# Gated linear attention and a squared-ReLU network on one core: float32 products by fewer sub-products, or by three single-pass products of exact parts

## The chip, the cores and the metric

The kernel runs on one NeuronCore of a Trainium2 chip. The metric is the device time of one execution in microseconds, lower is better. The profile gives a span a little shorter than that time: from the first to the last instruction of the core.

## The reference

Two stages follow each other. Inputs are four tensors of 4 batches, 8 heads, 768 steps and 48 channels in float32, and two weight matrices in float64 that the kernel itself turns into float32.

```python
for t in range(S):                                   # attention, S = 768
    state = alpha[:, :, t, :, None] * state + np.einsum('bhd,bhe->bhde', k[:, :, t], v[:, :, t])
    y[:, :, t] = np.einsum('bhd,bhde->bhe', q[:, :, t], state)
x = y.transpose(0, 2, 1, 3).reshape(B * S, H * D)    # 3072 tokens x 384
h = np.maximum(x @ w_in, 0.0)                        # 384 -> 2048
out = h * h @ w_out                                  # 2048 -> 384
```

The output is float32, 3072 x 384.

## The kernel before

Time is cut into 6 chunks of 128 steps. A block is one chunk of one batch, all heads, so there are 24 blocks. Four blocks, one of each batch, form a group of 512 tokens, and the feed-forward network runs group by group (g = 0 to 5). Attention of a group is made while the network of the group before runs.

*Attention of a block.* ACT takes the logarithm of alpha (`ln`), DVE splits it in two FP32R parts (`sp`, from block 8 on), TensorE sums the logs over time (`cs`, L267 and L268, FP32R matmuls of 384 columns), ACT makes exponentials (`eb`, `ei`), DVE scales q and k (`mq`, `mk`), TensorE transposes both (`turn`, L532) and ACT copies them (`turned_copied`, L540). Then `ga` and `gb` work on halves of 64 steps: `scores` (L421), `state_sums` (L447), masks and state updates on DVE, and the products y (L397). `ev` copies y from PSUM into x, the network's input.

*Feed-forward, group 0.* `ffn_in` and `ffn_out` are plain float32 matmuls (L723, 512 columns; L742, 384 columns). In this group the weights arrive and are converted from float64 on DVE and ACT.

*Feed-forward, groups 1 to 5.* `layer_in` follows a written list, LAYER. It computes the first layer with sub-products of sums of blocks: W_SUMS and X_SUMS say which blocks of the weights and of x are added or subtracted, a word such as `Pu0=w11x9` is one sub-product (two matmuls of 256 columns, L674), and words such as `u3=b1` or `u6=u3-b3` combine the results on ACT or DVE (L698, L616). The list has 40 sub-products where plain blocks would need 48. `ffn_product` does the same for the second layer with seven products instead of eight (PRODUCTS, L780, matmuls of 192 columns), with sums of weights (`tsum`) and of the hidden values (`sums`).

*Order of the work.* The schedule is manual: the order of the statements is the order of each engine's queue. `weave` goes through a list of units, each with a cost, and puts an event in when the sum of costs reaches the event's time. `attention` turns the table PLAN into events; in groups 1 to 4 they are all woven into `ffn_product`, with none in `layer_in`. PSUM has eight banks: `ps_att` holds four, `ps_ffn` four. x lives in one fixed buffer `x_t`, the hidden values in eight fixed buffers `hid`.

Of the kernel before, what the change touches and what calls it, by code (L numbers as in the profile page):

```python
# [17 lines left out]
GB = 4  # L18

# [6 lines left out]
def kernel(  # L26
# [25 lines left out]
    nc = tc.nc  # L52
# [16 lines left out]
    ps_att = ctx.enter_context(tc.tile_pool(name="ps_att", bufs=4, space=PSUM))  # L69
    ps_ffn = ctx.enter_context(tc.tile_pool(name="ps_ffn", bufs=GB, space=PSUM))  # L70
# [18 lines left out]
    w_in_t = consts.tile([128, NW, KM, DF // NW], FP32, name="w_in")  # L89
    w_in = [w_in_t[:, i] for i in range(NW)]  # L90
    w_out = [consts.tile([128, NJ // NW, DM], FP32, name=f"w_out{i}") for i in range(NW)]
    HM, NR2 = DM // 2, NJ // 4
    tsum = [kept(f"t{i}_", NR2, [128, 2, HM]) for i in (1, 2, 4)]
# [6 lines left out]
    lent = {("a", 2): flat(tsum[0][0]), ("a", 3): flat(tsum[0][1])}  # L100
    for x, n, i in (("q", 2, 6), ("q", 3, 7), ("k", 3, 5)):
        t = lent[x, n] = flat(w_out[i])[:, 0 : 64 * H].rearrange("a (h d) -> a h d", h=H)
        nc.gpsimd.memset(t[:, :, D:64], 0.0)
# [18 lines left out]
    def load_weights(i):  # L122
        dst = (w_in + w_out)[i]
        dt = moe_w_in.dtype
        raw = dst if dt == FP32 else raw_pool.tile(list(dst.shape), dt, tag="raw", name="raw")
        raws[i] = raw
        if i < NW:
            src = moe_w_in[:, i * DF // NW : (i + 1) * DF // NW]
            nc.sync.dma_start(out=raw, in_=src.rearrange("(k r) f -> r k f", r=128))
        else:  # L130
            i -= NW
            src = moe_w_out[i * DF // NW : (i + 1) * DF // NW, :]
            nc.sync.dma_start(out=raw, in_=src.rearrange("(j r) m -> r j m", r=128))
# [5 lines left out]

    def convert_first(i):  # L140
        if moe_w_in.dtype == FP32:
            return
        w = (w_in + w_out)[i].rearrange("a k f -> a (k f)")
# [4 lines left out]
        power = cv_pool.tile([128, n], U32, tag="power", name="power")  # L148
# [79 lines left out]
    x_t = consts.tile([128, KM, GB * C], FP32, name="x")  # L228
    xs_t = consts.tile([128, 11, HT], FP32, name="xs")
    hid = [consts.tile([128, 2, GB * C], FP32, name=f"hid{i}") for i in range(NJ // 2)]  # L230

    def bank(n, name, shape=(NP, C)):

        if n < GB and name in ("sc", "y"):
            return ps_ffn.tile([128, *shape], FP32, tag="f", name=name)
        return ps_att.tile([128, *shape], FP32, tag="att", name=name)
# [271 lines left out]
    def gb(a, n):  # L508
# [10 lines left out]
        if a is not None:  # L519
            ev(a)  # L520
            for m in (a, a + 1):
                blk[m].clear()
# [19 lines left out]
    def ev(n):  # L542
        g, t = divmod(n, GB)
        if t == 0:
            xT[g] = x_t
        x = xT[g].rearrange("a k (t c) -> a k t c", c=C)

        for p in range(NP):
            for e, f, end in ((1, 2 * p * D + 32, 2 * (p + 1) * D), (0, 2 * p * D, (2 * p + 1) * D)):
                copy = nc.vector.tensor_copy if n in SHARED and e else nc.scalar.copy  # L550
                r = 64 * (e ^ p % 2)
                while f < end:
# [3 lines left out]
                        out=x[to : to + m, kk, t : t + 2],  # L556
# [3 lines left out]
        blk[n].pop("y")  # L560

    def st(n):
# [25 lines left out]
    W_SUMS = """  # L588
        12=8+6 6=6-3 13=5-8 2=13-2 14=1-2 5=14+5 11=5+11 15=11-1 11=11+10 5=5+3 16=11+3 9=16+9
        3=8+3 10=9-10 1=1-10 17=11+4 4=4-14 18=0-1 0=3-0 19=11+7  # L590
    """
    X_SUMS = """
        6=4-0 7=6+5 8=1-7 9=8+3 10=4-2 11=10+5 12=5+4 13=9+6 14=3-11 15=14+1 16=9+2
    """

    LAYER = """
        Pu0=w11x9 Pv1=w8x6 Pu2=w8x6 u3=b1 Pv3=w3x7 v3=b2 Pv4=w11x9 u6=u3-b3 Pu5=w3x7 u1=u6+b4
        Pu6=w16x8 v3=v3-b5 Pu7=w13x5 u2=v3+b0 Pv4=w13x5 u5=b6-u2 Pv0=w16x8 u3=u5+b7 Pu6=w17x3  # L600
        v5=b0-u1 Pu7+w14x11 u0=v5+b4 Pu0=w5x12 u3=u3+b6 Pu5+w0x0 u7=v3-b7 v0=b0 Pv6=w17x3 V+u3
        Pu7+w2x10 v3=u0+b6 Pv1+w12x0 Rv3=+v3 u0=v0-b7 Pu6=w15x13 Qv3 u0=u0-b5 Pv4+w14x11 Ru0=+u0
        v0=u5+b6 Pu7+w1x15 Qu0 v2=u6-b4 Pu6+w9x16 u6=b7-u2 Pv5=w5x12 u6=u6-b0 Pv4+w2x10 u6=u6+b6
        u2=b5 Pu0+w4x2 Ru6=+u6 v4=u2-b4 Pu7+w10x14 Qu6 u2=u7+b0 Pv6=w15x13 Ru2=+u2 u7=v0+b7
        Pv4+w1x15 Qu2 v7=v5+b6 Pv3+w0x0 Ru7=-u7 u1=b4-u1 Pu7+w18x1 Qu7 v6=u1-b5 Pv1+w7x2 Su1
        Ru1=+b7 Pv4+w10x14 v0=v4-b3 Qu1 Pv6+w9x16 Rv4=+b1 V+v0 Pv5+w4x2 Qv4 v7=v7+b4 Pu2+w12x0
        v6=v6+b6 Rv7=-v7 v2=v2+b5 Pv0=w19x3 Qv7 V+v6 Rv2=+v2 Pv0+w6x1 Sv1 Qv2 Pu2+w7x2 v5=v5+b0
        Pu7=w19x3 Ru4=+b2 V+v5 Pu7+w6x1 Qu4 Pv4+w18x1 u5=u5+b7 V+u5 Rv1=+b4 Qv1 Su0 Sv0
    """
    FIRST = "u"  # L610

    acc, ws, sums = {}, {}, {}
# [5 lines left out]
    def parsed(text):  # L618
        for word in text.split():
            o, x, op, z = re.fullmatch(r"(\d+)=(\d+)([+-])(\d+)", word).groups()  # L620
            yield int(o), int(x), ALU.add if op == "+" else ALU.subtract, int(z)

    def w_slot(i):
        if i < 4 * KM:
            c, kk = divmod(i, KM)
            return w_in_t[:, 2 * c : 2 * c + 2, kk, :]
        r, i = divmod(i - 4 * KM, 3)
        if r not in ws:
            ws[r] = raw_pool.tile([128, 3, 2, 256], FP32, tag="raw", name="ws")
            if r == 2:  # L630
                sums.update({3: ws[r][:, 2]})
        return ws[r][:, i]

    def x_slot(i):
        kk, h = divmod(i, 2)
        return x_t[:, kk, h * HT : (h + 1) * HT] if kk < KM else xs_t[:, i - 2 * KM]

    w_sums = list(parsed(W_SUMS))

    def sum_w_in(i):  # L640
        o, x, op, z = w_sums[i]
        combine(((w_slot(o), w_slot(x), op, w_slot(z)),))

    def sum_x(g):
        if not xs_ready:
            a = raw_pool.tile([128, 3, 2, HT], FP32, tag="raw", name="s012")
            sums.update({r: a[:, r] for r in range(3)})
            xs_ready.append(True)
        for o, x, op, z in parsed(X_SUMS):
            combine(((x_slot(o), x_slot(x), op, x_slot(z)),))  # L650

    xs_ready = []

    def part(name):
        c, h = divmod(int(name[1]), 2)
        return hid[2 * c + "uv".index(name[0])][:, :, h * HT : (h + 1) * HT]

    def layer_in(g, between):
        banks = {}

        def operand(name):
            return banks[name[1]] if name[0] == "b" else part(name)

        for n, word in enumerate(LAYER.split()):
            if n in between:
                between[n]()
            if word[0] == "P":
                p, b, start, w, x = re.fullmatch(r"P([uv])(\d)([=+])w(\d+)x(\d+)", word).groups()
                if start == "=":
                    banks.pop(b, None)  # L670
                    pool, tag = ((ps_att, "att"), (ps_ffn, "f"))[int(b) // 4]
                    banks[b] = pool.tile([128, 2, HT], FP32, tag=tag, name="h")
                for i in range(2):
                    nc.tensor.matmul(  # L674
                        out=banks[b][:, i, :],
                        lhsT=w_slot(int(w))[:, "uv".index(p), i * 128 : (i + 1) * 128],
                        rhs=x_slot(int(x)), start=(start == "=" and i == 0), stop=True,
                        skip_group_check=True,
                    )
            elif word[0] == "S":  # L680
                r = 2 * int(word[2]) + "uv".index(word[1])
                combine(((sums[r], halves(r)[1], ALU.add, halves(NR2 + r)[1]),))
            elif word[0] == "V":
                t = part(word[2:])
                nc.vector.scalar_tensor_tensor(
                    out=t, in0=t, scalar=0.0, in1=t,
                    op0=ALU.max if word[1] == "+" else ALU.min, op1=ALU.mult,
                )
            elif word[0] == "Q":
                t = part(word[1:])  # L690
                nc.scalar.activation(out=t, in_=t, func=AF.Square)  # L691
            elif word[0] == "R":
                o, sign, x = word[1:3], word[4], word[5:]
                nc.scalar.activation(  # L694
                    out=part(o), in_=operand(x), func=AF.Relu, scale=1.0 if sign == "+" else -1.0
                )
            elif len(word) == 5:
                nc.scalar.copy(out=part(word[0:2]), in_=operand(word[3:5]))  # L698
            else:
                o, x, op, z = word[0:2], word[3:5], word[5], word[6:8]  # L700
                combine(((
                    part(o), operand(x), ALU.add if op == "+" else ALU.subtract, operand(z)
                ),))
# [272 lines left out]
```

## Time and profile before

| what | value |
|---|---|
| time, median of 3 executions | 551.77 us (548.78 to 1417.08) |
| profiled execution | 549.13 us, span 547.4 us |
| granted TensorE clock | 0.998 |
| PE busy | 534.2 us (98%) |
| DVE busy | 368.6 us (67%) |
| ACT busy | 235.8 us (43%) |
| moved by DMA | 37.02 MB, 108820 of 117085 packets under 512 B |

How to read the profile: busy time of PE counts a matmul from its start to its modelled end, so neighbours overlap, and the start-to-start distance is the true price of a matmul in a stream. A float32 matmul has two records, each with its load of weights (PEld). The slices cut the span into 40 equal parts and give the busy share in tenths. The chain of work follows back from the last instruction what released what. The five `layer_in` stages begin at 132.96, 222.97, 307.84, 392.34 and 472.28 us.

### The profile page before, as it was taken

What the parts mean: (1) busy time and instruction counts of PE and PEld (TensorE: products, weight loads), DVE (VectorE), ACT (ScalarE), POOL (GpSimd) and SP (SyncE); (2) the same over time, 40 slices, a digit from 0 to 9 for tenths busy, and PEclk for the clock granted to TensorE, in tenths of its full rate; (3) what the DMA queues carried; (4) which work ended last, traced back from release to release, by engine and by line L of the source; (5) the groups of instructions that cost most, each with busy time, mean ns of one, the idle gap of its engine ahead of it and who ended that gap; (6) DMA issues with size and microseconds to landing.
All of it is one profiled execution on the core that took longest, in us unless ns stands there. A gap on an engine that the chain in (4) does not pass through costs nothing.

```text
span 547.4 us, 12320 instructions
## 1 busy us (share of the span) xinstructions
PE 534.2 (98%) x5226; PEld 455.3 (83%) x5226; DVE 368.6 (67%) x656; ACT 235.8 (43%) x503; POOL 5.9 (1%) x26
## 2 busy tenths in 40 slices
PE   8889999999999999999999999999999999999996
PEld 5654456656889999989999988999988999988996
DVE  4888889993898873778583677673578651577530
ACT  4568874435264354246343236542326440336100
POOL 2010000000000000000000000000000000000000
PEclk9999999999999999999999999999999999999999
DMA  9979577201001664200343300252300000100001
GB/s 162 239 191 278 148 225 204 59 16 57 1 1 30 118 112 88 66 1 0 60 90 63 85 0 1 46 94 55 88 1 0 2 2 2 57 1 0 1 1 57
DMA packets 117085, 37.02 MB, mean 68 GB/s; under 512 B 108820, under 2 KB 111912, under 8 KB 117032
## 3 DMA queue, kind: packets, MB, share of 16 engines
q1 hardware_dynamic: 117032, 36.25, 29.5%
q8 instruction: 41, 0.67, 0.5%
q14 instruction: 12, 0.10, 0.1%
HBM read 31.49 MB, written 4.75 MB: 66 GB/s over the span
## 4 chain that ended last, share of the span: by engine, by line
PE 81%; DVE 10%; ACT 4%; issue 2%; DMA 2%; SPq 0%; POOL 0%; DVEq 0%; POOLq 0%
PE o L780 33%; PE h L674 32%; PE o L742 4%; PE y L397 4%; PE sckv L421 2%; PE T L532 2%; PE sckv L447 2%; ACT power L163 1%; DMA raw<-in_moe_w_in_dram 1%; DVE w_out L176 1%; DMA raw<-in_moe_w_out_dram 1%; DVE power L172 1%; DVE power L150 1%; DVE w_in L176 1%; DVE w_out L179 1%
## 5 line engine op out<-in xcount | busy, mean ns | idle before, releaser
L616 DVE TENSOR_TENSOR hid<-hid,h 128x512 f32<-128x512 f32 x130 | 88.4, 687 | 40.5 <-PE h L674 37.0
L780 PE MATMUL o<-w_out,hid 128*128 128x192 f32 x480 | 82.3, 327 | 0.0
L780 PEld LDWEIGHTS o<-w_out,hid 128*128 128x128 f32 x480 | 78.5, 190 | 0.6
L674 PE MATMUL h<-xs,w_in 128*128 128x256 f32 x320 | 74.8, 379 | 0.0
L555 ACT COPY x<-y 32x256 f32<-32x256 f32 (+2 forms) x132 | 46.3, 365 | 59.7 <-PE y L397 56.1
L674 PEld LDWEIGHTS h<-xs,w_in 128*128 128x128 f32 x320 | 60.7, 190 | 8.3
L674 PE MATMUL h<-x,ws 128*128 128x256 f32 x200 | 49.7, 379 | 0.0
L723 PE MATMUL h<-x,w_in 128*128 128x512 f32 (+1 forms) x108 | 43.5, 550 | 3.3 <-ACT x L555 1.8
L431 DVE COPY_PREDICATED am<-halves_mask,sckv 128x256 f32<-128x256 uint32 x40 | 15.5, 441 | 43.7 <-PE sckv L447 43.7
L698 ACT COPY hid<-h 128x512 f32<-128x512 f32 x20 | 11.7, 586 | 76.7 <-PE h L674 76.7
L780 PE MATMUL o<-t,s 128*128 128x192 f32 x240 | 43.2, 328 | 0.0
L742 PE MATMUL o<-w_out,hid 128*128 128x384 f32 x128 | 42.8, 490 | 0.0
L674 PEld LDWEIGHTS h<-x,ws 128*128 128x128 f32 x200 | 38.0, 190 | 5.2
L674 PE MATMUL h<-x,w_in 128*128 128x256 f32 x160 | 40.2, 379 | 0.0
L780 PEld LDWEIGHTS o<-t,s 128*128 128x128 f32 x240 | 39.5, 190 | 0.3
L723 PEld LDWEIGHTS h<-x,w_in 128*128 128x128 f32 x108 | 20.0, 190 | 23.4 <-issue 16.3
L742 PEld LDWEIGHTS o<-w_out,hid 128*128 128x128 f32 x128 | 23.9, 190 | 16.2 <-issue 0.5
L691 ACT ACTIVATE hid<-hid 128x512 f32<-128x512 f32 x55 | 34.7, 631 | 1.8
L674 PEld LDWEIGHTS h<-x,w_in 128*128 128x128 f32 x160 | 30.4, 190 | 4.1
L674 PE MATMUL h<-xs,ws 128*128 128x256 f32 x120 | 30.0, 379 | 0.0
L694 ACT ACTIVATE hid<-hid 128x512 f32<-128x512 f32 x35 | 22.0, 628 | 16.9 <-DVE hid L616 16.6
L780 PE MATMUL o<-t,hid 128*128 128x192 f32 x160 | 28.8, 331 | 0.0
(128 smaller groups left out, 764.8 us busy)
## 6 DMA issues: line engine op xcount, KB each, us to landing
raw<-in_moe_w_in_dram SPq DMA_DIRECT2D x8, 768.0 KB
raw<-in_moe_w_out_dram SPq DMA_DIRECT2D x8, 768.0 KB
v_in<-in_v_dram SPq DMA_DIRECT2D x24, 192.0 KB
out_dram<-osb SPq DMA_DIRECT2D x24, 192.0 KB
k_in<-in_k_dram SPq DMA_DIRECT2D x23, 192.0 KB
a_in<-in_alpha_dram SPq DMA_DIRECT2D x22, 192.0 KB
q_in<-in_q_dram SPq DMA_DIRECT2D x22, 192.0 KB
last<-row SPq DMA_DIRECT2D x40, 0.8 KB
```

What stands on the lines that cost most here:

```text
L176: nc.vector.scalar_tensor_tensor(out=w, in0=upper, scalar=2.0**-20, in1=w, op0=ALU.mult, op1=ALU.add)
L397: ins = nc.tensor.matmul(out=ys[e][64 * half : 64 * half + D + G * e, m % 2, p // 2, t], lhsT=lhsT, rhs=rhs, start=(half, e) not in seen, ...
L431: nc.vector.copy_predicated(out=am_h(n)[:, e, n % 2], data=ps[e][:, 0], mask=halves_mask.bitcast(U32).unsqueeze(1).to_broadcast([128, NP, ...
L555: copy(out=x[to : to + m, kk, t : t + 2], in_=blk[n]["y"][e][r : r + m, :, p // 2],)
L616: nc.vector.tensor_tensor(out=o, in0=x, in1=z, op=op)
L674: nc.tensor.matmul(out=banks[b][:, i, :], lhsT=w_slot(int(w))[:, "uv".index(p), i * 128 : (i + 1) * 128], rhs=x_slot(int(x)), start=(start ...
L691: nc.scalar.activation(out=t, in_=t, func=AF.Square)
L694: nc.scalar.activation(out=part(o), in_=operand(x), func=AF.Relu, scale=1.0 if sign == "+" else -1.0)
L698: nc.scalar.copy(out=part(word[0:2]), in_=operand(word[3:5]))
L723: nc.tensor.matmul(out=ps, lhsT=w[:, kk, c0 : c0 + 128], rhs=xT[g][:, kk, cols], start=(kk == 0), stop=(kk == KM - 1),)
L742: nc.tensor.matmul(out=acc[t][:, 0:DM], lhsT=hid[i][:, j, t * C : (t + 1) * C], rhs=w_out[i][:, j, :], start=(i == 0 and j == 0), stop=(i ...
L780: nc.tensor.matmul(out=acc[k][:, t, :], lhsT=lhs[:, j, t * C : (t + 1) * C], rhs=rhs[:, j, :], start=(first and r == R[0] and j + t == 0), ...
```

## The change

Both layers of the network give up the sub-products of sums. Each operand is cut into exact parts instead: a = x times (1 - 2^-13), written as FP32R[...], and l = x - a, the exact rest. For the weights b, the rest is scaled by 2^12, and d = b - l; for the moving or hidden side d = l - E a with E = 2^-12. Three passes, a with b, l with l and d with d, then give the product after scaling the first two by E: ACT reads the bank after the first two (`in_x`, Copy with scale E), the third pass adds to the bank, and DVE adds bank and copy (`in_y`). Each pass is a single-pass FP32R matmul of 512 columns in `in_passes` and of 384 columns in `of_tile`.

```diff
+    def in_x(j):
+        acc["h", j] = ps_ffn.tile([128, GB * C], FP32, tag="att", name="h")
+        in_passes(j, "b", "a", True, False)
+        in_passes(j, "l", "l", False, True)
+        hid[j] = two_k("hid")
+        nc.scalar.activation(out=hid[j], in_=acc["h", j], func=AF.Copy, scale=E)
+
+    def in_y(j):
+        in_passes(j, "d", "d", False, True)
+        combine(((hid[j], acc.pop(("h", j)), ALU.add, hid[j]),))
...
+    def split_to(a, l, x):
+        nc.scalar.activation(out=a, in_=x, func=AF.Copy, scale=NEAR)
+        combine(((l, x, ALU.subtract, a.bitcast(FP32)),))
+
+    def diff_to(d, a, l):
+        nc.vector.scalar_tensor_tensor(
+            out=d, in0=a.bitcast(FP32), scalar=-E, in1=l.bitcast(FP32), op0=ALU.mult, op1=ALU.add
+        )
...
+    def out_x(n):
+        p, jj = divmod(n, 2)
+        a, l = h_parts.pop(n)
+        for t in range(GB):
...
+            of_tile(t, a, here["b", "o", p][:, jj], start=n == 0)
+            of_tile(t, l, here["l", "o", p][:, jj], stop=n == NJ - 1)
```

The parts of the weights are made once: `cast_w`, `rest_w`, `scale_w` and `diff_w` are four steps (ACT, DVE, ACT, DVE) for each of 16 blocks of 128x768, four of them during group 0 and twelve during group 1. The parts l and d of a block are written to DRAM (`kept_parts`) and read again in each group by `pump`, which keeps up to nine tiles ahead; b stays in SBUF.

```diff
+    def pump():
+        while todo and sum(k[0] in "ld" for k in here) < room[0]:
+            key = todo.pop(0)
+            here[key] = wt("w" + key[0], FP32R, shapes[key[1]])
+            nc.sync.dma_start(out=words(here[key]), in_=kept_parts[key])
```

Because the parts of w_out are made during group 1, that group's second layer is plain float32, like group 0's (`plain_out`). All eight PSUM banks form one pool, and weights, hidden values and x take buffers from common pools as they come.

```diff
-    ps_att = ctx.enter_context(tc.tile_pool(name="ps_att", bufs=4, space=PSUM))
-    ps_ffn = ctx.enter_context(tc.tile_pool(name="ps_ffn", bufs=GB, space=PSUM))
+    ps_att = ctx.enter_context(tc.tile_pool(name="ps_att", bufs=8, space=PSUM))
+    ps_ffn = ps_att
...
+        weave(layer_in(g) + layer_out(g), events)
```

Attention's events are now woven over both layers, by the times in the table AT (`g1` for group 1, `g` for the later ones, `ga` and `gb` at 9 and 12 units), and `ev` is cut into four parts (`ev_part`), 0.8 units apart.

## The prediction

> **What bounds the kernel now.** I read the page's busy rows and slices first, then the costliest groups, then the busy table by stage, the chain in order of time, and last the timeline of TensorE and of its weight loads.
>
> Busy rows and slices of the kernel before:
> ```profile
> PE 534.2 (98%) x5226; PEld 455.3 (83%) x5226; DVE 368.6 (67%) x656; ACT 235.8 (43%) x503; POOL 5.9 (1%) x26
> ...
> PE   8889999999999999999999999999999999999996
> ```
> PE is busy from the fourth slice (41 us) to the end. A busy PE may still be an inefficient one, so the question is what each matmul costs from start to start. The stages, by core time in us (PE, PEld, DVE and ACT busy follow; group 2's two layers, then group 5's):
> ```profile
> 222.80:257.30 34.50, 34.50 (x162) 30.39 (x161) 26.34 (x42) 14.56 (x24) 0.00 (x0) 1.00 0.03 12
> 257.30:307.70 50.40, 50.25 (x810) 47.81 (x810) 30.67 (x67) 20.23 (x56) 0.00 (x0) 1.00 0.36 65
> ...
> 472.10:506.60 34.50, 34.50 (x162) 30.39 (x161) 25.59 (x40) 14.56 (x24) 0.00 (x0) 1.00 0.07 23
> 506.60:547.40 40.80, 36.61 (x225) 36.29 (x224) 12.52 (x21) 2.21 (x4) 0.00 (x0) 0.97 0.06 20
> ```
> In layer_in DVE is busy 26 of 34.5 us, in layer_out with attention 31 of 50: neither sets the pace. The chain gives the matmul counts:
> ```profile
> 472.28 34.53 PE h L674 x160
> 506.81 36.41 PE o L780 x224
> ```
> So layer_in is 160 records at 34.5/160 = 0.2158 us (256 columns) and layer_out without attention 224 records at 36.4/224 = 0.1625 us (192 columns). The waits of PE after 134 us add to 0.4 us: there is none to remove, only matmul time.
>
> Plain float32 layers appear in group 0; the chain has the o matmuls of L742 (384 columns, two records per matmul), whose last record is 0.49 us long:
> ```profile
> 108.25 9.23 PE o L742 x28
> 123.73 9.23 PE o L742 x28
> ```
> (9.23-0.49)/27 = 0.324 us per record, 0.326 in a longer timeline stretch. And one place already runs the type that the change uses everywhere, the sums of logs (timeline of PE, start and length in us):
> ```profile
> 346.29 0.34 PE L268 MATMUL cs<-lo,causal_r 128*128 128x384 f32 x1
> 346.46 0.34 PE L267 MATMUL cs<-hi,causal_r 128*128 128x384 f32 x1
> 346.64 0.34 PE L268 MATMUL cs<-lo,causal_r 128*128 128x384 f32 x1
> 346.82 0.65 PE L780 MATMUL o<-t,s 128*128 128x192 f32 x3
> ```
> One record per matmul (float32 has two), starts 0.1767 us apart ((346.82-346.29)/3) for 384 columns. The same spacing shows at 171.4 and 430.8 us. This row carries most of the forecast.
>
> **What the Trainium skill says.** (1) "FP8 and Floating Point Precision", TensorE Precision Notes: true FP32 takes four passes, the reduced form one read truncated to 22 bits. The trace agrees on the ratio: 2 x 0.326 us against 0.1767 for 384 columns is 3.7. (2) "TensorE: Matmul & The Clock Gate", Back-to-back issue gap: N/2.4 + 2.5 ns for an isolated stream, 216 ns at 512 and 162.5 at 384. The trace agrees for float32 records (0.2158 for 2x256, 0.1625 for 2x192) and not for FP32R at 384 columns, 14 ns longer. The measurement decides. (3) The same page, Step-by-step: loads of weights are pulled ahead of running matmuls. The trace agrees: the loads of cs start with the matmul before.
>
> **The change part by part.** Groups 1 to 5, PE alone first.
>
> Layer_in: 160 records go, 16 x 3 x 3 = 144 FP32R matmuls of 512 columns come. No row shows this size. Low end: the page's 0.2158, so 31.1 us. High end: 0.1767 scaled by 512/384, 0.2356, so 33.9 us. The excess of 14 ns taken as fixed gives 0.230. I take the middle of the ends, 0.2257: 32.5 us, a saving of 34.5-32.5 = 2.0 us, five times: 10.0 us (3.0 to 17.0).
>
> Layer_out of groups 2 to 5: 224 records go, 16 x 4 x 3 = 192 FP32R matmuls of 384 columns come. At the measured 0.1767: 33.9 us, saving 2.5 us, four times: 10.0 us. If long streams reach 0.1625: 31.2 us, 20.8 us in all.
>
> Layer_out of group 1 falls back to plain float32: 64 matmuls, 128 records x 0.326 = 41.7 us against 36.4: a loss of 5.3 us.
>
> PE sum: 10.0 + 10.0 - 5.3 = 14.7 us saved (7.7 to 32.5). Attention's matmuls are the same ones; group 2's layer_out with them is 50.4 against 36.4, 14 us, unchanged.
>
> Group 0 keeps its float32 layers. Its W_SUMS (20 DVE operations, 0.69 us) make way for four weight blocks of two DVE and two ACT operations of about 0.95 and 0.9 us. PE is full from 41 us on in group 0, so both lie beside it: zero. The tail (last add, store) is the same: zero.
>
> Work on the other engines. A float32 DVE operation on 128x512 takes 0.69 us, ACT about 0.6. Layer_in of group 2 or 3 now has on ACT 16 evictions, 8 x 2 Relu/Square, 3 splits (21 us) plus attention, by the instruction order of the changed kernel 34 us between its first and last eviction, against 36 us of PE there; DVE has 31 of 37. T copies come 0.26 us apart on ACT where one lasts 0.41, so the 34 is nearer 30. In group 1's layer_in, where four weight blocks are still made, DVE sums to 31.2 us against PE's 31 to 33. Layer_out: each out_x is 8 x 0.1767 = 1.41 us of PE and needs two DVE operations, 1.38 us; they start five units ahead, so they just keep up.
>
> New waits. in_y(n) adds to the bank that ACT must have read first (the Copy by E); the slack is in_x(n+1), in_y(n-1), in_x(n+2), about 3.3 us, and eight T copies and a Relu/Square pair ahead of it on ACT take 2.1 + 1.3. Behind a waiting in_y all of PE waits. PSUM is one pool of eight: T takes four banks, y two, h three or four, so in_x or scores wait for the copies and masks that free a bank. cs to T has 4.1 us of PE between (0.7 + 1.4 + 0.7 + 1.4), where the chain of before had 5.2 (262.1 to 267.3) with no wait. No row shows these waits. Low end zero, as before. High end, 2.5 us for each of the 8 pairs of blocks and 6 in group 1: 26 us. I take 1 us a pair and 2 for group 1: 10 us.
>
> Transfers: parts l and d are 32 x 0.39 = 12.6 MB per group from 2 on, fetched nine tiles ahead (some 17 us). A group lasts about 78 us, so 160 GB/s, plus some 4 MB of attention. The slices of before reached 278 GB/s with float64 weights and small packets mixed: hidden, I think.
>
> Sum: span 547.4 - 14.7 + 10 = 542.7. Reported times lie 1.7 us (profiled run, 549.1) to 4.4 us (median) over the span; with 3 that is 545.7, say 545.
>
> **The rivals.** *Fast stream*: FP32R runs at the page's rate in long streams, and cs is slow only because it stands between float32 matmuls. For: float32 obeys that rate to the ns. Against: four spacings in a row at 0.1767. 547.4 - 32.5 + 10 + 3 = 528.
> *Side engines set the pace*: ACT and DVE at 85 to 100% of PE in layer_in, eight shared banks and in-order queues turn into waits of 26 us, and 512 columns cost 0.2356: 547.4 - 7.7 + 26 + 3 = 569, slower. For: the sums above. Against: the evictions have 3 us of slack and the layer_outs leave ACT time.
> *Parts come late*: if parts and attention's 192-byte packets share 193 GB/s (the first 40 us), a group's 16.6 MB takes 86 us against 78, 8 us late in each of groups 2 to 4. Of these 24 us some 10 would overlap the waits already counted: 545 + 14 = 559. Against: the later slices with small packets alone still reach 118 GB/s while mostly idle.
>
> **How the numbers follow.** Main forecast 0.43, fast stream 0.30, side engines 0.19, late parts 0.08. The range 524 to 563 takes in the first two, most of the late parts and a mild form of the third. Two per cent are 541 and 563. Faster: the fast stream and a quarter of the main case (512 columns near 0.2158, or few waits), 0.40. Slower: most of the third and some of the fourth, 0.20. Within: 0.40.
>
> **What would show it.** Right: starts of FP32R matmuls 0.177 us apart at 384 columns and 0.216 to 0.236 at 512; group 5's layer_in near 32.5 us, its layer_out near 34, group 1's layer_out 5 us longer than before; some 10 us of PE waiting for ACT copies, DVE adds or banks, mostly in layer_in of groups 1 to 3; DMA never last before an in_x. Wrong: 0.1625 and 0.2158 (fast stream); PE waits over 20 us; PE waiting for wl or wd.

## The result, and the profile after

| | before | after |
|---|---|---|
| time, median (lowest to highest) | 549.85 us (548.78 to 551.77) | 529.84 us (529.18 to 531.26) |
| span of the profiled execution | 547.4 us | 527.9 us |

The ratio is 0.9635, 95% interval 0.9594 to 0.9676: 3.65% faster. The forecast of 545 us was 1.2% below the 551.77 us that stood in the table of before. One execution of the kernel before, at 1417 us, is left out as disturbed.

The page of the changed kernel, busy rows, slices and the DMA queue that carries the parts:

```profile
PE 516.0 (98%) x4922; PEld 412.0 (78%) x4922; DVE 362.7 (69%) x611; ACT 319.8 (61%) x654; POOL 6.1 (1%) x26
...
PE   8889999999999999999999999999999999999997
...
q1 hardware_dynamic: 140072, 99.17, 67.5%
```

PE is as full as before, with 304 records fewer. ACT went from 236 to 320 us, DVE stayed (369 to 363), and the moved bytes rose from 37 to 100 MB. So the gain again has to be read from what a matmul costs and from what PE waits for, not from busy shares.

The table by stage, for group 2's two layers and group 5's (columns as in the table of before):

```profile
224.30:268.80 44.50, 44.50 (x635) 36.78 (x634) 30.13 (x58) 35.26 (x79) 0.00 (x0) 1.00 0.89 236
268.80:303.70 34.90, 34.90 (x289) 34.58 (x289) 25.92 (x43) 14.32 (x32) 0.00 (x0) 1.00 0.64 195
...
458.10:490.80 32.70, 32.70 (x146) 27.05 (x146) 17.41 (x28) 19.12 (x34) 0.00 (x0) 1.00 0.90 306
490.80:527.90 37.10, 33.45 (x193) 33.13 (x191) 21.63 (x35) 9.94 (x19) 0.00 (x0) 0.99 0.13 46
```

Most of attention has moved into layer_in: that stage of group 2 now has 635 records and lasts 44.5 us. PE is busy for every microsecond of it, with ACT at 35.3 us (79%) and DVE at 30.1 us (68%).

The chain in order of time (start, length, what): the end of group 0, the first line of each layer_in, and all of group 5:

```profile
121.69 9.23 PE o L853 x28
130.92 6.86 PE h L696 x30
...
224.49 6.18 PE h L696 x27
...
303.83 6.17 PE h L696 x27
...
383.07 6.17 PE h L696 x27
...
458.26 32.68 PE h L696 x144
490.94 33.32 PE o L762 x192
```

Group 5 has both layers without attention: layer_in fell from 34.53 to 32.68 us, layer_out from 36.41 to 33.32. Group 1 begins at 130.92 us, where before it was 132.96. From the starts of the layer_ins in this chain and the end of the last matmul (490.94 + 33.32 = 524.26) the groups last, in us:

| group | before | after | change |
|---|---|---|---|
| 1 | 90.0 | 93.6 | +3.6 |
| 2 | 84.9 | 79.3 | -5.5 |
| 3 | 84.5 | 79.2 | -5.3 |
| 4 | 79.9 | 75.2 | -4.7 |
| 5 | 70.9 | 66.0 | -4.9 |

That is -16.9 us. Group 0 gives 2.0 and the tail 0.5 (3.6 us after the last matmul, where it was 4.2): together the 19.5 us between the spans.

What a matmul costs, from the timeline of PE. First layer_in (512 columns; pieces of three matmuls each), then layer_out (384 columns):

```profile
470.38 0.84 PE L696 MATMUL h<-xd,wd 128*128 128x512 f32 x3
471.06 0.84 PE L696 MATMUL h<-xa,wb 128*128 128x512 f32 x3
471.74 0.84 PE L696 MATMUL h<-xl,wl 128*128 128x512 f32 x3
...
494.79 0.33 PE L762 MATMUL o<-wl,hl 128*128 128x384 f32 x1
494.96 0.33 PE L762 MATMUL o<-wb,hx 128*128 128x384 f32 x1
495.14 0.33 PE L762 MATMUL o<-wl,hx 128*128 128x384 f32 x1
495.31 0.33 PE L762 MATMUL o<-wb,hx 128*128 128x384 f32 x1
```

Three matmuls of 512 columns take 0.68 us, 0.2267 each. Those of 384 columns start 0.1733 us apart ((495.31-494.79)/3), not 0.1767.

And what PE waits for from 130 us to the end (us in total, times, longest); these are all the entries of PE itself, first of the changed kernel, then of the kernel before (from 134 us on):

```profile
PE y L413 <- issue: 0.5, 1, 0.5
...
PE cs L283 <- DVE hi L271: 0.4, 1, 0.4
```
```profile
PE sckv L421 <- issue: 0.2, 1, 0.2
PE sckv L447 <- issue: 0.2, 1, 0.2
```

0.9 us, against 0.4 before. Of the 10 us of new waits in the forecast, 0.5 came. That is the largest part of the miss, and the experiments ask why.

### The profile page after: what moved, and what is told of

Its sections match the earlier page's. It is cut to its first block, busy times and chain, and to the rows that moved or that the text cites. A ratio compares the mean times of both kernels' runs of the same rounds, so it can differ in the third digit from the quotient of the medians.

```text
span 527.9 us, 12213 instructions
## 1 busy us (share of the span) xinstructions
PE 516.0 (98%) x4922; PEld 412.0 (78%) x4922; DVE 362.7 (69%) x611; ACT 319.8 (61%) x654; POOL 6.1 (1%) x26
## 3 DMA queue, kind: packets, MB, share of 16 engines
q1 hardware_dynamic: 140072, 99.17, 67.5%
## 4 chain that ended last, share of the span: by engine, by line
PE 85%; DVE 5%; DMA 3%; ACT 2%; SPq 2%; issue 2%; DVEq 0%
PE h L696 32%; PE o L762 25%; PE o L853 13%; PE y L413 4%; PE h L833 3%; PE sckv L437 2%; PE T L544 2%; PE sckv L463 2%; DMA raw<-in_moe_w_in_dram 1%; SPq L318 1%; DMA a_in<-in_alpha_dram 1%; SPq L122 1%; DVE w_in L194 1%; DMA lo<-wl 1%; PE cs L284 1%
## 5 line engine op out<-in xcount | busy, mean ns | idle before, releaser
L709 ACT ACTIVATE hid<-h 128x512 f32<-128x512 f32 x80 | 47.1, 593 | 71.1 <-PE h L696 71.0
L629 DVE TENSOR_TENSOR hid<-h,hid 128x512 f32<-128x512 f32 x80 | 54.5, 688 | 41.8 <-PE h L696 38.0
L853 PEld LDWEIGHTS o<-w_out,hid 128*128 128x128 f32 x256 | 47.7, 190 | 31.5 <-issue 0.5
L696 PE MATMUL h<-xa,wb 128*128 128x512 f32 x240 | 68.5, 394 | 0.0
L696 PE MATMUL h<-xd,wd 128*128 128x512 f32 x240 | 68.5, 398 | 0.0
L696 PE MATMUL h<-xl,wl 128*128 128x512 f32 x240 | 67.7, 390 | 0.0
L696 PEld LDWEIGHTS h<-xl,wl 128*128 128x128 f32 x240 | 45.0, 188 | 9.8
L696 PEld LDWEIGHTS h<-xa,wb 128*128 128x128 f32 x240 | 44.9, 188 | 9.8
L762 PE MATMUL o<-wd,hd 128*128 128x384 f32 x256 | 45.0, 334 | 0.0
L762 PEld LDWEIGHTS o<-wd,hd 128*128 128x128 f32 x256 | 44.4, 188 | 0.0
```

What stands on the lines that cost most here:

```text
L629: nc.vector.tensor_tensor(out=o, in0=x, in1=z, op=op)
L696: nc.tensor.matmul(out=acc["h", j], lhsT=here[w, "i", p][:, kk, jj * 128 : (jj + 1) * 128], rhs=x_parts[x][:, kk], start=start and kk == 0 ...
L709: nc.scalar.activation(out=hid[j], in_=acc["h", j], func=AF.Copy, scale=E)
L762: nc.tensor.matmul(out=acc[t][:, 0:DM], lhsT=lhs[:, t * C : (t + 1) * C], rhs=rhs, start=start, stop=stop, skip_group_check=True,)
L853: nc.tensor.matmul(out=acc[t][:, 0:DM], lhsT=hid[per * i + j][:, t * C : (t + 1) * C], rhs=w_out[i][:, j, :], start=(i == 0 and j == 0), s ...
```

## Experiments

In the expectations, A is the theory that I held for that step and B its rival. Times are medians, each with its ratio to the kernel before on the same chip in the same session (549.23 us for the first four, 549.65 for the last four). Spans are compared with the 527.9 us of the changed kernel.

### The pool of eight banks: does it take the waits away?

```diff
-    ps_att = ctx.enter_context(tc.tile_pool(name="ps_att", bufs=8, space=PSUM))
-    ps_ffn = ps_att
+    ps_att = ctx.enter_context(tc.tile_pool(name="ps_att", bufs=4, space=PSUM))
+    ps_ffn = ctx.enter_context(tc.tile_pool(name="ps_ffn", bufs=4, space=PSUM))
```

> The changed kernel with PSUM split again, four banks for attention and four for the network, as before the change. Theory A (the gain is matmul time alone; the handoffs have slack and PE waits for nothing from group 1 on): with four banks for h, y and sckv back on their own four, two or three h tiles fit and at most small waits appear, 530 to 533 us. Theory B (the common pool is what keeps the waits away that I forecast, about 1 us for each pair of blocks and more in group 1): 538 to 545 us, with PE idle before sckv, T or h for a freed bank.

Measured: 535.33 us, ratio 0.9757 (0.9741 to 0.9773), span 533.5, 5.6 us longer. Waits of PE and its loads that are new, from 128 us on:

```profile
PEld h L696 <- DVE hid L629: 5.6, 8, 1.4
PE h L696 <- DVE hid L629: 2.8, 4, 1.0
```

The result lies between the two expectations. With four banks, `in_x` waits for a bank that the last add (`in_y`) has yet to free. So a wait for banks is real, and the common pool removes it: the forecast counted the pool as a source of waits, and it is the reverse. It accounts for 4.6 us, about half of what was forecast: four of the five layer_ins are 1.0 to 1.7 us longer. The other 1.0 of the 5.6 us lies in group 0.

### The order: in_y directly behind its in_x

```diff
-        for n in range(NJ + 2):
+        for n in range(NJ + 0):
...
-            if 0 <= n - 2 < NJ:
-                units.append((0.53, in_y, (n - 2,)))
+            if 0 <= n - 0 < NJ:
+                units.append((0.53, in_y, (n - 0,)))
...
```

> The changed kernel with the third pass right behind the first two (in_y(n) after in_x(n) instead of after in_x(n+2)), so PE has no slack for ACT's eviction. Theory A (the forecast waits did not come because 3.3 us of slack hides them): each of the 80 third passes now waits for the eviction, some 0.2 us to notice, 0.59 us to copy, plus ACT's queue: 64 us and more, 590 to 620 us. Theory B (there is hardly anything to hide, since TensorE can write the bank while ACT reads or the eviction is early): under 540 us.

Measured: 596.14 us, ratio 1.0861 (1.0822 to 1.0899), span 596.0. The waits, and two pieces of the timeline in group 5 (at the end of the line: idle before it, and what ended that):

```profile
PEld h L696 <- ACT hid L709: 74.9, 70, 1.7
PE h L696 <- ACT hid L709: 46.3, 63, 1.3
```
```profile
549.02 0.96 PE L696 MATMUL h<-xd,wd 128*128 128x512 f32 x3 [0.69 <-ACT hid L709]
...
552.04 0.96 PE L696 MATMUL h<-xd,wd 128*128 128x512 f32 x3 [0.69 <-ACT hid L709]
```

One block now takes 3.02 us where its nine matmuls take 2.04: 0.98 us lost. The view shows only 0.69 of it as idle, because it counts from the modelled end of the matmul before; from start to start the third pass comes 0.85 us late, and it takes 0.13 us longer itself (0.96 us for three matmuls against 0.84). This is the bare price of the wait that the change adds: the trip from PE to ACT's copy (0.60 us) and back. Over all 80 third passes the five layer_ins are 66.1 us longer, 0.83 each, since pieces of attention fill some of the waits. (Of the other 2 us, 3.3 were lost in group 0, which the edit leaves as it was and where the granted clock was 0.50 from 24 to 28 us, and 1.3 gained in group 1's layer_out.) In the changed kernel the trip is paid in the shadow of other matmuls.

### Half the slack: one block between

```diff
...
-            if 0 <= n - 2 < NJ:
-                units.append((0.53, in_y, (n - 2,)))
+            if 0 <= n - 1 < NJ:
+                units.append((0.53, in_y, (n - 1,)))
...
```

> The changed kernel with the third pass one step behind instead of two: in_y(n) follows in_x(n+1), so about 1.35 us of PE work lies between the end of the second pass and the third. With no slack at all the wait was 0.83 us for each (66 us in 80). Theory A (the slack is needed only for the bursts on ACT's queue, eight T copies or a Relu/Square pair ahead of the eviction): the bare wait of 0.83 us is hidden, the bursts of 1.3 to 3.4 us are not, some two per pair of blocks and one per second j: 5 to 15 us more, 535 to 545 us. Theory B (ACT has no bursts that matter): 530 us.

Measured: 533.60 us, ratio 0.9712 (0.9676 to 0.9749), span 531.9: 4.0 us longer than with two. The five layer_ins are 0.7 to 1.1 us longer each.

```profile
PEld h L696 <- ACT hid L709: 5.6, 9, 0.9
PE h L696 <- ACT hid L709: 1.7, 5, 0.5
```

Slightly less than A expected. Between `in_x(n)` and `in_y(n)` PE now has one `in_y` and one `in_x`: 0.68 + 1.36 = 2.04 us. That leaves about 1.1 us over the trip of 0.83 to 0.98, and bursts on ACT go beyond it a few times: in the trace a pair of Relu and Square (1.3 us), copies of y or a split stands just ahead of the eviction that PE waits for. With two blocks between, the work in between is `in_y(n-2)`, `in_x(n+1)`, `in_y(n-1)`, `in_x(n+2)`: 4.08 us. The forecast left the first of these out and came to 3.3.

### How far from the bound is ACT?

Two more Relu on each hidden block, which change no value:

```diff
     def in_post(j):
         h = hid[j]
+        for _ in range(2):
+            nc.scalar.activation(out=h, in_=h, func=AF.Relu)
```

> The changed kernel with two more Relu operations on each hidden tile (repeating Relu changes no value), 2 x 16 x 0.6 us = 20 us more ACT work in each layer_in; ACT was busy 35 of 44.5 us in layer_in of group 2. Theory A (ACT has a reserve of some 9 us per layer_in and the attention events and evictions queue behind the rest): groups 1 to 4 each lose about 8 to 12 us and group 5, with 19 of 33 us busy, little: 560 to 580 us. Theory B (the hidden tiles' Relu and Square are late enough to be put off into layer_out, where ACT is 14 of 35 us busy): under 540 us.

Measured: 577.95 us, ratio 1.0510 (1.0493 to 1.0528), span 576.2: 48.3 of the 100 us that ACT got (160 x 0.63) became time.

```profile
PE h L696 <- ACT hid L709: 14.3, 16, 2.8
PE h L696 <- DVE us L474: 5.3, 3, 1.8
PEld h L696 <- ACT hid L709: 22.0, 20, 3.2
```

The wait that I forecast does come, once ACT is full. The arithmetic is that of a sum: group 2's layer_in has ACT busy 35.3 of 44.5 us, so 9.2 us free; 20.2 us are added, 11 too many, and layer_in grew by 7.5 and layer_out by 2.7 us. In group 5 ACT has 19.1 of 32.7 us; 20.2 more give 39.3, and layer_in became 39.8, where A had expected little. ACT has a reserve of 9 to 14 us in the layer_ins of groups 2 to 5, and PE waits for none of its evictions in the changed kernel.

The sum is not quite clean. Behind the four longest waits, of 1.8 to 2.8 us, the granted clock fell: to 0.63 from 176 to 180 us, 0.71 from 260 to 264, 0.61 from 348 to 352 and 0.65 from 536 to 540. Summed over these stretches and their neighbours, 4 us times what the clock lacks of 1 gives an estimate of at most 7 us of the 48.3 for that.

### How far from the bound is DVE in layer_out?

```diff
-        diff_to(h_diff[n], *h_parts[n])
+        for _ in range(2):
+            diff_to(h_diff[n], *h_parts[n])
```

> The changed kernel with each diff_h made twice, the same values, so DVE has three operations of 0.69 us for each hidden tile of groups 2 to 5 instead of two: 2.07 us against 8 x 0.173 = 1.38 us of PE per out_x. Theory A (DVE paced layer_out to within its lead of five tiles, as the forecast had it: 1.38 against 1.38): PE waits for hl in the second half of each layer_out, 13 x 2.07 = 26.9 us of DVE against 22 us of PE: about 4 to 6 us in each of four groups, 546 to 555 us. Theory B (DVE has room, and the five units of lead take it up): under 533 us.

Measured: 559.36 us, ratio 1.0169 (1.0132 to 1.0205), span 559.6, 31.7 us longer.

```profile
PE o L763 <- DVE hl L629: 8.7, 20, 1.3
...
PE o L763 <- DVE hx L629: 7.7, 17, 0.9
...
PEld o L763 <- DVE hl L629: 15.1, 20, 1.6
...
PEld o L763 <- DVE hx L629: 13.1, 17, 1.2
```

In the four layer_outs concerned, 13 blocks each get their difference there (the other three are made in layer_in): 4 x 13 x 0.69 = 36 us more for DVE. These layer_outs grew by 7.2, 6.3, 6.3 and 7.5 us (group 2's from 35.05 to 42.2), 27 us together. The direction was A's, the size larger than A gave. Here the margin is about 2 us per layer_out ((36 - 27) / 4): two DVE operations of 0.69 us stand against 8 x 0.1733 = 1.39 us of PE.

The other 4.8 us lie in group 1's layer_out, where the edit changes nothing. DVE waited there until a part of the weights was stored and its buffer free, PE waited behind DVE, and then the granted clock fell, where it is 1.00 in the changed kernel (idle time at the end of the line; in the third line the clock is the third number from the end):

```profile
187.57 0.96 DVE L629 TENSOR_TENSOR wl<-w_out,wb 128x768 fp32r<-128x768 f32 x1 [2.09 <-DMA lo<-wl]
```
```profile
189.66 0.41 PE L283 MATMUL cs<-hi,causal_r 128*128 128x384 f32 x1 [2.00 <-DVE us L474]
```
```profile
190.00:200.00 10.00, 9.52 (x34) 5.24 (x34) 6.87 (x11) 6.66 (x15) 0.00 (x0) 0.66 0.66 201
```

### Are the transfers a limit?

Four tiles of parts ahead instead of nine in groups 2 to 4:

```diff
-        room[0] = AT["room1" if g == 1 else "room"]
+        room[0] = AT["room1"] if g == 1 else 9 if g == NG - 1 else 4
```

> The changed kernel with four instead of nine tiles of weight parts in SBUF or on their way in groups 2 to 4 (group 5 keeps nine). Theory A (a part comes 3 to 4 us after its issue, and the nine tiles, some 17 us ahead, are far more than needed): PE waits for wl or wd only a little, 530 to 535 us. Theory B (transfers share the queue with attention's small packets and are as close as the rival in the forecast said): 545 us and more, with PE waiting for DMA.

Measured: 532.02 us, ratio 0.9685 (0.9651 to 0.9718), span 529.8, 1.9 us longer. The intervals of the two ratios overlap (0.9594 to 0.9676 for the changed kernel), so only the trace tells them apart.

```profile
PE h L696 <- DMA wd<-di: 1.3, 3, 0.5
```

With less than half of the lead the parts are late three times, by 0.5 us at most. With nine, PE never waits for one. The rival with late parts is out.

The other direction is closer to its limit. While the parts are made and stored, DVE waits for a store before it can use the buffer again; this is the changed kernel from 130 us on:

```profile
DVE wl L629 <- DMA lo<-wl: 3.5, 4, 1.6
```

Its chain runs from such a store (181.83 us) over DVE to the 0.4 us that PE waits before `cs` at 189 us.

### The price of an FP32R matmul

This kernel leaves the whole computation out and stores zeros. It runs streams of 30 FP32R matmuls, four weight blocks and four banks in turn, and streams of 12 float32 matmuls between.

```python
stream("r512", st_r, mov_r, 512, 30)
stream("f512", st_f, mov_f, 512, 12)
stream("r384", st_r, mov_r, 384, 30)
stream("f384", st_f, mov_f, 384, 12)
...
stream("r384 one bank", st_r, mov_r, 384, 30, nb=1)
stream("r384 one weight", st_r, mov_r, 384, 30, nst=1)
```

> A kernel that leaves the whole computation out and stores zeros: streams of 30 FP32R and 12 float32 matmuls back to back, no other engine at work. Start to start at 512 and 384 columns the changed kernel showed 0.2258 and 0.1727 us, the sums of logs 0.1767. Theory A (a fixed extra per FP32R matmul, about 13 ns over columns/2.4 GHz): 0.226, 0.173, 0.120 and 0.066 us at 512, 384, 256 and 128 columns, the same with one bank. Theory B (an extra in proportion, by read bandwidth): 0.226, 0.169, 0.113, 0.056. Theory C (other engines' traffic causes it): 0.2158 and 0.1625 here. One weight block used by all, as in the sums of logs: 0.177 if the reused block makes that row slow, 0.173 if not.

Its timeline of PE (whole streams, start and length; float32 has two records per matmul):

```profile
17.89 7.41 PE L53 MATMUL b<-movr,str 128*128 128x512 f32 x30
25.14 10.46 PE L53 MATMUL b<-movf,stf 128*128 128x512 f32 x24
35.03 5.79 PE L53 MATMUL b<-movr,str 128*128 128x384 f32 x30
...
48.10 4.05 PE L53 MATMUL b<-movr,str 128*128 128x256 f32 x30
...
56.98 3.65 PE L53 MATMUL b<-movr,str 128*128 128x128 f32 x30
```

A whole stream holds the changeover from one type to the other, so the price is read from the distances of the starts inside. Over the later part of each stream these are, in us:

| columns | FP32R, one record | float32, each of two records |
|---|---|---|
| 512 | 0.2267 | 0.4292 |
| 384 | 0.1733 | 0.3225 |
| 256 | 0.1200 | 0.2158 |
| 128 | 0.1115 | 0.1115 |

From 256 to 512 columns a column of FP32R costs (0.2267 - 0.1200) / 256 = 0.4167 ns, which is 2.4 columns per ns, so the columns alone are 0.1067, 0.1600 and 0.2133 us, and each matmul costs 0.0133 us more, always the same. So the excess is fixed per matmul, neither proportional to the columns nor absent in a long stream; one bank or one weight block changes nothing (0.1733). At 128 columns none of the expectations holds: 0.1115 where A had 0.066. The fast stream, as a rival, is out.

The first distances of the 384-column stream, behind the one of the changeover, were 171, 175, 178, 185, 175 and 182 ns before it settled at 173. Group 5's layer_out in the changed kernel opens with the same six. The sums of logs, four matmuls that follow others, look like this in the changed kernel:

```profile
309.84 0.34 PE L283 MATMUL cs<-hi,causal_r 128*128 128x384 f32 x1
310.01 0.34 PE L284 MATMUL cs<-lo,causal_r 128*128 128x384 f32 x1
310.19 0.34 PE L283 MATMUL cs<-hi,causal_r 128*128 128x384 f32 x1
310.37 0.34 PE L284 MATMUL cs<-lo,causal_r 128*128 128x384 f32 x1
```

Their 0.1767 lies among the distances of a run that has just begun, and that was the row on which I based 192 matmuls in a row. That the beginning is the reason is not shown: the sums of logs share one weight block, and the stream with one weight block settled at once.

### Where group 0's 2 us come from

An edit of the kernel *before* alone: the sums of weights, W_SUMS, are issued later in group 0.

```diff
-    events += [(36 + i, sum_w_in, (i,)) for i in range(len(w_sums))]
+    events += [(44 + 0.75 * i, sum_w_in, (i,)) for i in range(len(w_sums))]
```

> The kernel before with one edit: the 20 W_SUMS of group 0 begin at 44 units and come 0.75 apart, instead of from 36 units 1 apart. In group 0 the changed kernel reached layer_in of group 1 2.4 us earlier (130.4 against 132.8 us). Theory A (W_SUMS stood on DVE ahead of the masks and state updates for which the next scores wait, and that wait is gone): the start of layer_in moves to 130.5 to 131.5 us and the time falls by 1.5 to 2 us. Theory B (the gain comes from the weight conversion's wider pool or elsewhere): no change, 132.8 us.

Measured: 547.23 us, ratio 0.9967 (0.9958 to 0.9977), 2.0 us less. The first line of its chain in group 1:

```profile
130.94 34.53 PE h L674 x160
```

130.94 us, where the kernel before had 132.96 and the changed one has 130.92. What stood in the way is on DVE's queue in the kernel before, and ends in a wait of PE:

```profile
104.11 0.69 DVE L616 TENSOR_TENSOR w_in<-ws,w_in 128x512 f32<-128x512 f32 x1
104.83 0.69 DVE L616 TENSOR_TENSOR ws<-w_in 128x512 f32<-128x512 f32 x1
105.44 0.77 DVE L431 COPY_PREDICATED am<-halves_mask,sckv 128x256 f32<-128x256 uint32 x2
106.10 0.42 DVE L458 TENSOR_TENSOR us<-sckv,s 128x256 f32<-128x256 f32 x1
```
```profile
106.66 1.07 PE L421 MATMUL sckv<-qs,ks 48*64 48x64 f32 x29 [0.98 <-DVE us L458]
```

The masks of attention and the update of the state wait behind sums that nobody needs until group 1. In the changed kernel, with W_SUMS gone, the masks start at 102.38 us and PE is busy for all of 95 to 109 us (12.9 of 14.0 before). The wait costs more than the 0.98 us that the view shows: from the y matmuls before it (104.99 us) to the next o (108.18) it is 3.19 us, in the changed kernel 1.56 (104.58 to 106.14).

## Why the prediction was right or wrong

The forecast was a span of 542.7 us; it is 527.9. The 14.8 us, by the forecast's own steps (changes in us):

| step of the forecast | forecast | measured | difference |
|---|---|---|---|
| layer_in of groups 1 to 5, 512 columns at 0.2257 | -2.0 each | -1.85 each | +0.7 |
| layer_out of groups 2 to 5 at 0.1767 | -2.5 each | -3.1 each | -2.4 |
| group 1's layer_out in float32, and attention | +5.3, 0 | +4.2 in all | -1.1 |
| new waits | +10 | +0.5 | -9.5 |
| group 0 | 0 | -2.0 | -2.0 |
| tail | 0 | -0.5 | -0.5 |

The two layers are measured in group 5, without attention; the third row is what is left of the 19.5 us. The stream's 0.3225 us gives 128 x 0.3225 = 41.3 us for group 1's layer_out, +4.9, so some 0.7 us less for attention, which no run here takes apart.

**The step that failed is the one of new waits: "I take 1 us a pair and 2 for group 1: 10 us".** The trace has 0.9 us of waits where the kernel before had 0.4. The mechanism is real: with no block between, each third pass costs 0.83 us on average. But the size had no row under it, as the forecast says, and two parts of the working were wrong. The slack was counted as 3.3 us; it is 4.1, since `in_y(n-2)` also lies in it. Even the forecast's own 3.3 us would have hidden nearly all: the run with 2.0 us of slack lost only 4.0 us. And ACT's 34 us between its first and last eviction, "nearer 30", were set against 36 us of PE; in group 2 ACT is busy there for 30.4 of 39.3 us (225.92 to 265.21), 77% and not 94%. The pool of eight was counted among the causes of waits; with two pools of four the kernel is 5.6 us slower.

**Layer_out was mis-sized by one row.** "At the measured 0.1767" took four matmuls that stand between others (three distances, not "four spacings in a row") for the price of a stream. The stream measured 0.1733: 0.6 us per layer_out. The Trainium skill's page "TensorE: Matmul & The Clock Gate" gives N/2.4 + 2.5 ns under Back-to-back issue gap, as the gap of an isolated matmul, from which 0.1625 us for 384 columns is an estimate; for a stream it gives less, about 131 ns at 512 columns. FP32R measured N/2.4 + 13.3 ns here, 227 ns at 512. So FP32R agrees with neither figure, and the fixed excess, which the forecast named (0.230 at 512), was the right form.

**Group 0 at zero was wrong.** "Both lie beside it" looked at PE's fullness by slice (in tenths) and overlooked PE's one wait there, which the view shows as 0.98 us and which costs 1.6. The late sums show that 2.0 us came from there.

What was right: layer_in at 32.5 us (32.7), with some luck, since it was the middle of two ends and rested on no row; group 1, +3.3 us without its waits (+3.6); DVE in layer_out just keeping up (two times 0.69 against 1.39 us, and three quarters of the doubled difference turned into time); parts hidden behind PE (no DMA wait at nine tiles ahead). The forecast's 3 us between span and reported time is 1.9 in this kernel.

The rivals: *fast stream* gave 528 us, nearest to the 529.8, but its mechanism is refuted: neither 0.1625 nor 0.2158 appears. It hit by luck: it counted 32.5 us of matmul time saved where about 17 were, 15 too many, and against that some 13 us too much: 9.5 of waits that did not come, nothing for group 0 and the tail, and 1.1 between span and reported time. *Side engines set the pace* is refuted for this kernel (0.9 us of waits), and the run with more work on ACT shows what it would have looked like and how near it is. *Parts come late* is refuted by the lead of four tiles.

Open: why some FP32R runs begin with slower matmuls and others don't (of the four streams of 384 columns two, one weight block and every matmul with its own start, settled at once). Not tried: parts of w_out early enough that group 1's second layer uses three passes too. By estimate it would take about 8 us from PE (41.3 to 33.3), but DVE is busy 64 of 94 us in that group and would get 32 more operations of 0.69 us, 22 us, so it would be full.

## What to carry to other kernels

A wait that is added on the critical engine costs nothing if the work placed between the two halves is longer than the trip (here 0.83 to 0.98 us) and the other engine's burst together; count all the work that the written order puts there, then compare the other engine's sum with the whole stage, including what else the stage has taken on. Price a stream from a stream: a short run between other matmuls, even if it looks the same each time, need not have that price. Work on an idle engine that is needed late can still cost time if it stands in that engine's queue ahead of something needed now: look at the queue, not at the busy share.

## What the runs showed of the hardware that I had not expected

- In the streams an FP32R matmul cost 0.4167 ns a column and 13.3 ns more, from 256 to 512 columns; at 128 columns it was 0.1115 us, and a float32 record of 128 columns the same 0.1115.
- A run of FP32R matmuls at 384 columns can begin with six distances of 171 to 185 ns before it settles at 173, in the stream and in group 5's layer_out alike.
- The way from a matmul's end over an ACT copy of 128x512 to the next matmul on the same bank cost PE 0.83 us on average, 0.98 where no other matmul lay between.
- No slowdown of the matmuls by 63 MB more of transfers (67.5% of the time of 16 DMA engines in all) is to be seen: in the stage with 306 GB/s a matmul of 512 columns costs 0.2267 us, as in the stream with nothing beside it.
- In the runs with more work on ACT and on DVE the granted clock fell, from group 1 on, right behind each wait of PE of 1.8 to 2.8 us (five times, to 0.61 to 0.71 over the following 4 or 10 us), and not behind waits of up to 1.7 us. In the run with more work on DVE group 1's layer_out had 1.8 us more of waits and was 4.8 us longer.
